# Head normalised tile by tile, query weights loaded in two parts, output matmuls started on their first inputs, and more zero-weight matmuls in a two-layer attention and gMLP kernel

## The chip, the cores and the metric

The kernel runs on one core of a Trainium2 chip. The metric is the device time of one launch in microseconds (us). I quote medians of several launches. One profiled launch per kernel gives the trace; its span is about 1.8 us shorter than the time of the same launch. TensorE runs the matmuls, whose results land in a memory called PSUM; ScalarE computes exponentials and other table functions, VectorE and GpSimd do elementwise work, and DMA queues move data. Copying a result out of PSUM is called eviction.

## The reference, cut to what matters

```python
# S = 2048 tokens, D = 512, H = 32 heads of Dh = 16, one shared K and one shared V head
def attention(x):                       # layernorm(x) comes in
    q, k, v = x @ wq, x @ wk, x @ wv
    p = softmax(q_h @ k.T * Dh**-0.5)   # 32 heads, 2048 x 2048 each
    return concat_heads(p @ v) @ wo
def mixer(x):                           # F = 1792, Fh = 896
    z = gelu(x @ w_in)
    z1, z2 = z[:, :Fh], layernorm(z[:, Fh:])
    g = w_sp @ z2 + b_sp[:, None]       # spatial 2048 x 2048 matmul ("gating")
    return (z1 * g) @ w_out
for _ in range(2):                      # two layers
    x = x + attention(layernorm(x))
    x = x + mixer(layernorm(x))
```

The work is dominated by 2 x 32 x 2048 x 2048 exponentials.

## The kernel before

The kernel builds a fixed instruction order for each engine, with its own list scheduler, before anything runs. The scheduler works with modelled durations and with the priorities in the code (a lower `prio` goes first); on the chip each engine runs its list in order and waits on semaphores. So a small edit of a priority or a dependency can move instructions far away from the place of the edit.

Most exponentials are computed on ScalarE, about 500 blocks of them on VectorE by a polynomial. After each chunk of queries ScalarE switches its function table to gelu and back; I call this a gelu stall. TensorE has a clock that drops after idle time (a stretch table below shows it fall to 0.50), and the kernel fills its idle time with matmuls whose weights are zero. I call the three places where the exponentials do not run back to back the seams: the head, the end of layer 0 and the end of layer 1.

The loading of the weights, with the clears of padded buffers on GpSimd (`pm` is a GpSimd memset):

```python
lq = self.dma(lambda e: e.dma_start(wq_nat, A_wq.rearrange(...)), (), "ldq", 524288, 1.2, "act")
for p in range(8):
    ld_x(p)                                   # 8 pairs of 128-row tiles of x, on the other queue
# ... cut ...
m = pm(self.wk_rep[:], 0.0, 512, 0.4)         # then a ScalarE copy of wk into it
m = pm(self.wv_rep[:], 0.0, 512, 0.5)         # then a ScalarE copy of wv into it
m = pm(self.wq_pad[:], 0.0, 4096, 0.6)
self.c_wq = sc.op("act", ... ACTF.Copy of all 2048 elements of wq ..., [m, lq], 1.2)
m = pm(self.V[:], 0.0, 2048, 0.7)
```

The keys: tiles are normalised two at a time, and all K and V matmuls of a pair are one job (`ln` also computes the reciprocal roots, on GpSimd):

```python
ts = (2 * p, 2 * p + 1)
ev = self.ln(ts, ...)
# ... cut ...
_, (k, v) = sc.job([(pe, 4 * d_mm(256) + 8 * d_mm(128))], [...], [ev, self.c_wk, self.c_wv], 1.0)
```

The end of a layer: for each of eight output blocks of 256 rows, gating matmuls for seven feature tiles in four groups, then eviction, addition and multiplication, then output matmuls that wait for all of them:

```python
for tc in range(8):
    hs = []
    for f0 in range(0, NF, 2):
        # ... gating matmuls (cut) ...
        pl, (ev,) = sc.job(pieces, [dict(... tensor_copy ..., prio=1.1, ...)], ...)
        ad = sc.op("dve", ... ALU.add ..., [ev] + ..., 0.9)
        ev = sc.op("dve", ... ALU.mult ..., [ad, zld], 0.9)
        hs.append(ev)
    for tt in range(2):
        ks = [(0, 1), (2, 3), (4, 5, 6)]
        pl, (xo,) = sc.job([... output matmuls, one piece for each of ks ...],
                           [... residual addition ...], hs + [self.l_wout], pr - 0.3)
```

The zero-weight matmuls: `peek` offers one only when the next unit of attention is neither at the end nor exactly at the half (the seam between the layers), and not before `wo` has been loaded:

```python
def peek(self, f):
    if u >= len(k.units) or u == len(k.units) // 2 or k.l_wo.start is None or k.c_zero.start is None:
        return None
    f = max(f, k.l_wo.vis, k.c_zero.vis)
```

The softmax here doesn't subtract the row's maximum and nothing guards it: scores larger than these inputs give would overflow.

## Time and profile before

The median of three launches was 1889.84 us (1886.19 to 1890.11).

| | of 1887.9 us |
|---|---|
| ScalarE busy | 93% |
| VectorE busy | 93% |
| TensorE busy | 85% |
| mean granted TensorE clock | 0.979 |
| first exponential | 18.3 us |
| last exponential of layer 0, first of layer 1 | 887.9, 932.7 us |
| last exponential of layer 1 | 1825.9 us |

These are whole lines of the page of the profile before: the busy times of the engines, the chain of work that ended last by engine, and two groups (ScalarE's exponentials and the zero-weight matmuls). In a group line the figures after the bar are busy us, mean ns of one, and the idle time before it with what ended it.

```profile
PE 1613.0 (85%) x12178; PEld 497.1 (26%) x12178; DVE 1750.5 (93%) x3129; ACT 1763.4 (93%) x1570; POOL 58.2 (3%) x101
...
ACT 35%; PE 26%; DVE 25%; issue 13%; POOL 1%; ACTq 0%; POOLq 0%
...
L1288 ACT ACTIVATE Pa<-ps_all 128x1536 bf16<-128x1536 f32 (+1 forms) x1440 | 1642.9, 1345 | 33.4 <-PE ps_all L1559 28.7
...
L1545 PE MATMUL ps_all<-wo_r,zero 128*128 128x512 bf16 x818 | 256.2, 391 | 0.6 <-DVE E L1464 0.2
```

Two engines are busy 93% of the time. Inside the attention the share is higher: from 100 to 200 us ScalarE is busy 100.0 us and VectorE 98.8. So the attention stretches are nearly full, but for the gelu stalls. What can be had without touching them is in the seams. The timeline of the head before (start us, length us, engine, line, operation, and in brackets the idle time before it with what ended it):

```profile
2.34 3.51 POOL L566 MEMSET wq_pad<- 128x4096 bf16 x1
...
5.79 1.80 POOL L566 MEMSET V<- 128x2048 bf16 x1
...
7.89 0.72 POOL L602 TENSOR_TENSOR rs<-ve,mhalf 128x2 f32<-128x2 f32 x1
...
10.08 1.91 ACT L582 ACTIVATE wq_pad<-z1s 128x2048 bf16<-128x2048 bf16 x1 [4.70 <-DMA z1s<-in_A_wq_dram]
...
14.63 3.28 PE L739 MATMUL ps_all<-xnTA,wq_pad 128*128 128x512 bf16 x8
...
18.29 2.36 ACT L1288 ACTIVATE Pa<-ps_all 128x1536 bf16<-128x1536 f32 x2 [1.11 <-PE ps_all L1559]
21.67 44.98 ACT L1288 ACTIVATE Pa<-ps_all 128x1536 bf16<-128x1536 f32 x39 [1.01 <-PE ps_all L1559]
```

GpSimd clears buffers until 7.6 us, and only then computes the first reciprocal root, on which the first normalised tile waits. The eight query matmuls take 3.28 us.

The chain of waits through the last seam before (start us, length us, engine, tile, line):

```profile
1837.06 3.18 PE ps_all L875 x8
...
1847.47 7.66 PE ps_all L1123 x28
...
1858.91 6.23 PE ps_all L1123 x28
1865.17 0.69 DVE X L1128
1865.86 0.60 DVE E L1102
1866.71 0.42 DVE E L1105
...
1868.59 0.30 DVE E L1108
1868.93 6.23 PE ps_all L1123 x28
```

L875 is a group of the last chunk's input matmuls, L1123 the output matmuls of two blocks. TensorE works 6.23 us, then waits 3.8 us through a chain of VectorE work, and the next two blocks begin 10.02 us after the last (1858.91 to 1868.93).

The stretch table around one gelu stall of layer 1 before. Of each line I use the stretch, its length, the first busy time (TensorE, with its count), the fourth (ScalarE) and the number before the last two, which is the granted clock:

```profile
1454.00:1462.00 8.00, 7.69 (x36) 3.25 (x34) 5.99 (x9) 7.99 (x4) 0.00 (x0) 1.00 0.01 2
1462.00:1465.00 3.00, 0.00 (x0) 0.00 (x0) 0.00 (x0) 3.00 (x1) 0.00 (x0) 0.95 0.00 0
1465.00:1470.00 5.00, 0.00 (x0) 0.00 (x0) 2.52 (x6) 4.97 (x3) 0.00 (x0) 0.50 0.33 107
```

The zero-weight matmuls of this stall run at its start, because nothing makes them wait. Then TensorE idles, from 1461.7 us on in the timeline, and some 3.0 us later its clock falls to half: the 0.95 is 2.7 us at full clock and 0.3 at half.

### The profile page before, as it was taken

The numbers are of one execution on the slowest core, as the hardware profiler recorded it, in microseconds if no ns is written. First come the engines' busy times: TensorE is split into PE (matmuls) and PEld (weight loads), VectorE is DVE, ScalarE is ACT, GpSimd is POOL, SyncE is SP. The second block draws the span as 40 slices with busy tenths as digits, with TensorE's granted clock in tenths as the row PEclk, the third lists the DMA queues.
The fourth block names the chain that finished last, engine by engine and source line by source line (L and its number), as shares of the span: only waits on it lengthen the run. The fifth ranks groups of instructions, "written<-read, shape, count | busy, mean of one in ns | idle before, by whom it ended". The sixth has DMA issues, their size and how long they took to land.

```text
span 1887.9 us, 30817 instructions
## 1 busy us (share of the span) xinstructions
PE 1613.0 (85%) x12178; PEld 497.1 (26%) x12178; DVE 1750.5 (93%) x3129; ACT 1763.4 (93%) x1570; POOL 58.2 (3%) x101
## 2 busy tenths in 40 slices
PE   7877888788889998989888778888888899999987
PEld 3222222122222232222432222222222223223233
DVE  7999999999889999997869999999999799989977
ACT  7999999999999999998579999999999999999973
POOL 3000000000000000000100000000000000000000
PEclk9999999999999999999999999999999799989999
DMA  9900000000010101011110000000000100011213
GB/s 254 232 1 1 1 1 1 1 1 1 5 36 23 46 1 43 24 55 45 54 33 1 1 1 1 1 1 1 1 1 1 40 23 23 1 43 35 66 45 109
DMA packets 85448, 59.17 MB, mean 31 GB/s; under 512 B 39476, under 2 KB 81720, under 8 KB 85304
## 3 DMA queue, kind: packets, MB, share of 16 engines
q1 hardware_dynamic: 83720, 56.64, 10.6%
q8 instruction: 97, 1.59, 0.4%
q10 hardware_dynamic: 1584, 0.56, 0.1%
q14 instruction: 47, 0.39, 0.1%
HBM read 30.97 MB, written 17.83 MB: 26 GB/s over the span
## 4 chain that ended last, share of the span: by engine, by line
ACT 35%; PE 26%; DVE 25%; issue 13%; POOL 1%; ACTq 0%; POOLq 0%
ACT Pa L1288 32%; PE ps_all L1036 7%; PE ps_all L1559 7%; PE ps_all L1363 4%; DVE E L1464 4%; DVE Pd L1502 3%; PE ps_all L1123 2%; DVE E L1500 2%; DVE E L1491 2%; DVE E L1497 2%; PE ps_all L1545 1%; DVE st L596 1%; ACT z2n L943 1%; DVE z2n L886 1%; DVE E L1494 1%
## 5 line engine op out<-in xcount | busy, mean ns | idle before, releaser
L1288 ACT ACTIVATE Pa<-ps_all 128x1536 bf16<-128x1536 f32 (+1 forms) x1440 | 1642.9, 1345 | 33.4 <-PE ps_all L1559 28.7
L1559 PE MATMUL ps_all<-qs,kT 32*128 32x512 bf16 x4096 | 567.9, 390 | 206.4 <-ACT Pa L1288 193.4
L1464 DVE TENSOR_SCALAR E<-ps_all 128x512 int32<-128x512 f32 x499 | 339.7, 684 | 24.0 <-PE ps_all L1559 22.5
L1559 PEld LDWEIGHTS ps_all<-qs,kT 32*128 32x128 bf16 x4096 | 139.4, 91 | 754.6 <-ACT Pa L1288 674.5
L1363 PE MATMUL ps_all<-Pa,V 128*32 128x512 bf16 x3597 | 324.3, 391 | 0.1
L1502 DVE SCALAR_TENSOR_TENSOR Pd<-E 128x1024 uint16<-128x1024 int32 x250 | 303.4, 1214 | 0.9
L1545 PE MATMUL ps_all<-wo_r,zero 128*128 128x512 bf16 x818 | 256.2, 391 | 0.6 <-DVE E L1464 0.2
L1036 PE MATMUL ps_all<-wsT,z2n 128*128 128x512 bf16 x714 | 198.9, 388 | 3.5 <-DVE gp L1048 2.4
L1363 PE MATMUL ps_all<-Pd,V 128*32 128x512 bf16 x499 | 176.6, 390 | 0.0
L1497 DVE TENSOR_TENSOR E<-E 128x1024 f16<-128x1024 f16 x250 | 170.9, 684 | 3.3
L1500 DVE TENSOR_TENSOR E<-E 128x1024 f16<-128x1024 f16 x250 | 170.4, 682 | 1.9
L1491 DVE TENSOR_SCALAR E<-E 128x1024 f16<-128x1024 uint16 x250 | 170.9, 684 | 1.3
L1493 DVE TENSOR_SCALAR E<-E 128x1024 f16<-128x1024 f16 x250 | 104.6, 418 | 2.2
L1494 DVE TENSOR_SCALAR E<-E 128x1024 f16<-128x1024 f16 x250 | 104.3, 417 | 2.1
L1545 PEld LDWEIGHTS ps_all<-wo_r,zero 128*128 128x128 bf16 x818 | 62.2, 97 | 132.1 <-issue 105.0
L1363 PEld LDWEIGHTS ps_all<-Pa,V 128*32 128x32 bf16 x3597 | 63.6, 94 | 121.5 <-issue 113.7
L1048 DVE TENSOR_TENSOR gp<-ps_all,gp 128x512 f16<-128x512 f32 x112 | 75.5, 685 | 20.3 <-PE ps_all L1036 20.0
L1036 PEld LDWEIGHTS ps_all<-wsT,z2n 128*128 128x128 bf16 x714 | 55.5, 98 | 100.3 <-issue 54.5
L739 PE MATMUL ps_all<-xnTA,wq_pad 128*128 128x512 bf16 (+2 forms) x384 | 71.0, 314 | 1.8 <-DVE E L1464 1.3
L875 PE MATMUL ps_all<-w_in_r,xnTB 128*128 128x448 bf16 x256 | 64.9, 365 | 4.6 <-DVE xnTB L628 1.7
L1123 PE MATMUL ps_all<-E 128*128 128x512 bf16 x224 | 55.2, 396 | 12.3 <-DVE E L1108 12.1
L911 PE MATMUL ps_all<-xnTB,w_in_r 128*128 128x512 bf16 (+2 forms) x336 | 61.8, 310 | 3.7 <-DVE z1s L922 1.9
(85 smaller groups left out, 1087.6 us busy)
## 6 DMA issues: line engine op xcount, KB each, us to landing
wsT_scratch<-gp SPq DMA_DIRECT2D x16, 512.0 KB, 4.0
wsT<-wsT_scratch SPq DMA_DIRECT2D x8, 1024.0 KB, 5.3
z1s<-z_scratch SPq DMA_DIRECT2D x16, 448.0 KB, 4.0
wsT<-wsT_scratch SPq DMA_DIRECT2D x8, 512.0 KB, 3.5
z_scratch<-z1s SPq DMA_DIRECT2D x4, 896.0 KB, 6.3
X<-in_A_x_dram SPq DMA_DIRECT2D x8, 256.0 KB, 7.5
out_dram<-X SPq DMA_DIRECT2D x16, 128.0 KB, 1.8
w_in_r<-in_B_w_in_dram SPq DMA_DIRECT2D x1, 1792.0 KB, 12.1
```

The source lines that it names most:

```text
L1036: ins = e.matmul(self.b32(b), self.z2n[:, s, f * 128:(f + 1) * 128], w_[:, s - s0, :], start=st, stop=sp)
L1288: return e.activation(k.Pa[:, base:base + n, :], k.b32(b0, n).rearrange("p (k q) -> p k q", k=n), ACTF.Exp, scale=SCALE)
L1363: ins = e.matmul(k.b32(k.pvb)[32 * j:32 * j + 32, :], k.V[:, u.kt, 32 * j:32 * j + 32], b.slot, tile_position=(0, 32 * j), start=u.first, ...
L1464: return k.sc.op("dve", lambda e: e.tensor_scalar(k.eI[:, s, 512 * i:512 * (i + 1)], k.b32(j.bank.idx)[:, 0:512], C_LOG2, C_BIAS, op0=ALU. ...
L1491: return lambda e: e.tensor_scalar(out, a, m, None, op0=ALU.mult)
L1493: return lambda e: e.tensor_scalar(out, a, b, None, op0=ALU.add)
L1494: return lambda e: e.tensor_scalar(out, a, m, b, op0=ALU.mult, op1=ALU.add)
L1497: o4 = sc.op("dve", lambda e: e.tensor_tensor(q, u, w, ALU.mult), d_sb(n, 0.521e-3), [o3], pr)
L1500: o6 = sc.op("dve", lambda e: e.tensor_tensor(q, q, u, ALU.mult), d_sb(n, 0.521e-3), [o5], pr)
L1502: o7 = sc.op("dve", lambda e: e.scalar_tensor_tensor(po.bitcast(U16), I, 2.0 ** -9, q, op0=ALU.mult, op1=ALU.add), d_sb(n, 1.042e-3), [o6] ...
L1545: return e.matmul(k.b32(k.pvb if b is None else b.idx), k.zero[:], k.wo_r[:, 0, :], start=b is not None, stop=b is not None)
L1559: return e.matmul(self.b32(bank), self.kT[32 * j:32 * j + 32, kt * 128:(kt + 1) * 128], self.qs[32 * j:32 * j + 32, g.q.slot, :], tile_pos ...
```

## The change

The intent is to shorten the three seams: start the exponentials sooner, keep TensorE's clock up where it had been left to fall, and let the output matmuls of a layer's end begin before all their inputs are there. The diff, cut to its core (cut are: lent PSUM banks at the start, the new helpers, the split of the K and V matmuls into two jobs for the first two pairs, query matmuls that wait for their own part of wq alone, and the addition of epsilon on VectorE instead of GpSimd in the normalisations at the ends of the layers):

```diff
 # load: wq in two parts, clears on VectorE (vm) instead of GpSimd (pm)
-lq = self.dma(... wq_nat ..., "ldq", 524288, 1.2, "act")
+lq = [ld_q(0, 128, "act")]
 for p in range(8):
     ld_x(p)
+    if p == 3:
+        lq.append(ld_q(128, 512, "sp"))
-m = pm(self.wq_pad[:], 0.0, 4096, 0.6)
-self.c_wq = sc.op("act", ... copy of 2048 elements ..., [m, lq], 1.2)
-m = pm(self.V[:], 0.0, 2048, 0.7)
+m = vm(self.wq_pad[:], 4096, 0.11)                       # wk_rep, wv_rep likewise
+c0 = rows(wqv[:, :, 0:8, :], wqn[:, :, 0:8, :], m, lq[0], 512, 1.2)               # ScalarE
+c1 = rows(wqv[:, :, 8:32, :], wqn[:, :, 8:32, :], m, lq[1], 1536, 3.0, "pool")    # GpSimd
+m = vm(self.V[:], 2048, 0.13)
 # layer_keys: the first four tiles one by one, first in priority
-ev = self.ln(ts, ..., 1.0)
+pr = 0.3 if p < 2 else 1.0
+for tt in ([ts[:1], ts[1:]] if p < 2 else [ts]):
+    evs.append(self.ln(tt, ..., dd, pr, p < 2))          # urgent: + eps on VectorE
 # closing: earlier block first, output matmuls start on the first feature tiles
-... prio=1.1 ... / 0.9 / 0.9
+... prio=1.1 + 0.01 * tc ... / 0.9 + 0.01 * tc / 0.89 + 0.01 * tc
-    dur=d_psum(512), prio=0.8, deps=[...])], hs + [self.l_wout], pr - 0.3)
+    dur=d_psum(512), prio=0.8, deps=[...])], [self.l_wout], pr - 0.3,
+    piece_deps=[hs[0:1], hs[1:2], hs[2:4]], soft=evs)
 # WarmStream.peek: also before the first scores and at the ends of the layers
-if u >= len(k.units) or u == len(k.units) // 2 or k.l_wo.start is None or k.c_zero.start is None:
+if sc.nleft == 0 or k.c_zero.start is None:
     return None
-f = max(f, k.l_wo.vis, k.c_zero.vis)
+f = max(f, k.c_zero.vis)
 # ... and the moving operand is zeros too, so wo need not have been loaded
-return e.matmul(..., k.zero[:], k.wo_r[:, 0, :], ...)
+return e.matmul(..., k.zero[:], k.zero[:, None, :].to_broadcast([P, 4, P]), ...)
```

## The prediction

> **What bounds the kernel now.** The page's busy table gives ScalarE 93% and VectorE 93% of 1887.9 us, TensorE 85%. The chain of waits gives ScalarE 35% (nearly all exponentials), TensorE 26%, VectorE 25%: two attention stretches in which exponentials run back to back (busy 99-100% in the stretch table), joined by three seams where they do not run: the head (0-22 us), the end of layer 0 (about 860-980) and the end of layer 1 (about 1825-1888). The change leaves the attention loop alone and works on the seams. By the instruction order VectorE's exponential blocks go from 499 to 497, zero-weight matmuls from 818 to 882.
>
> **Head.** In the timeline the first exponential starts at 18.3 us, with another ScalarE gap of 1.0 us ending at 21.7. The chain there is a 3.5 us clear of wq on GpSimd, a 1.8 us clear of V, which delays the first reciprocal root to 7.9 us, then pairwise normalisation, and a 1.9 us wq copy on ScalarE ending at 12.0, in front of the first key evictions. TensorE is cold: eight query matmuls take 3.28 us, 1.89 later. Now the clears move to VectorE before X lands (3.9 us), tiles go one at a time, only a quarter of wq is waited for, and fourteen zero-weight matmuls warm TensorE from about 1 us. My estimate from these durations: four tiles need some 1.3 us of VectorE each, so the last is ready near 10 us, then queries (1.8) and eviction (0.6): first exponential at 13-14 us. Gain about 5 us, and all later work shifts with it.
>
> **End of layer 1.** Each two output blocks take 10.02 us: output matmuls 6.23 busy, then 3.7 us of eviction, addition and multiplication during which TensorE waits. VectorE interleaves both blocks, so both become ready late. Now the earlier block has priority and output matmuls start on the first two feature tiles. VectorE work per two blocks, from issue spacing: 4.8 us of add and multiply, 2.4 of residual adds, 0.6 of eviction, 7.8 in all; TensorE needs about 7.6. I expect about 8.5 per two blocks, 5-6 us over four. The warm clock should bring the eight gating matmuls from 3.18 us (clock 0.67 there) to about 1.6, and the first output group from 7.66 to 6.2. Together about 8 us.
>
> **End of layer 0.** The same edits, but the gating matmuls are already warm (1.69) and VectorE is 97-100% busy during 915-925 with the next layer's statistics; the gain is the cold output group (7.90 us, clock 0.83) and earlier starts: about 3-4 us.
>
> **Not expected to change.** The gelu stalls: in 1450-1500 the clock is 0.80, because 34 zero-weight matmuls run at once and TensorE then idles 8.6 us. The change gives them no wait that would pace them. The Trainium skill ("TensorE: Matmul & The Clock Gate", section on what is happening) says about 3.4 us of idleness halves the clock; this trace agrees (0.50 from 1465).
>
> **Sum:** 5 + 8 + 3.5, about 16.5 us of 1890, less than 1%. I predict 1873 us, 80% range 1862 to 1883. Chances: faster by over 2% 0.03, within 2% 0.96, slower 0.01.
>
> **Shown right by:** first exponential at 13-14 us; matmuls before it at full clock; last output blocks every 8-9 us; gating matmuls of layer 1 near 1.6 us; unchanged clock dips at the gelu stalls; unchanged mean of exponentials.
>
> **Wrong if:** keys for later tiles arrive late and return the head's gain as ScalarE gaps before 40 us; the zero-weight matmuls delay real ones; GpSimd's long wq copy delays a reciprocal root or slows VectorE; or the reshuffled static order shifts the cold clock after gelu stalls by some us either way.

## The result, and the profile after

| | before | after |
|---|---|---|
| median, us | 1889.97 of 4 | 1877.49 of 4 |
| range, us | 1886.19 to 1890.75 | 1875.62 to 1878.77 |
| profiled launch: span, us | 1887.9 | 1873.8 |
| mean granted clock of it | 0.979 | 0.989 |

The ratio is 0.9937, with a 95% interval of 0.992 to 0.9954: within 2%, and faster by 12.5 us of the medians. A ratio here is the mean time of one kernel's runs over that of the other's of the same rounds, so it is not quite the ratio of the medians that I quote. The profiled launch of after was the fastest of its four, so the two spans differ by 14.1 us.

To see where the time came from, I cut both traces at ScalarE's exponentials: the start of the 41st (the start-up is over by then), the last of layer 0, the 41st of layer 1, the last of layer 1, and the end.

| stretch, us | before | after | difference, of unrounded times |
|---|---|---|---|
| head, to the 41st exponential | 64.9 | 60.9 | -4.0 |
| rest of layer 0's attention | 823.0 | 824.9 | +1.9 |
| seam between the layers, to the 41st exponential of layer 1 | 112.8 | 109.6 | -3.3 |
| rest of layer 1's attention | 825.2 | 823.7 | -1.5 |
| last seam | 62.0 | 54.8 | -7.2 |

The differences add up to -14.1. The three seams give 14.5 us, and the attention between them changes by +0.4 in sum. At the 41st exponential of the head both kernels have done the same work (100 blocks on ScalarE and 8 on VectorE), so the mark is fair. Head and last seam repeat within some tenths of a us between kernels that have the same order there; the attention stretches do not, and the seam between the layers moves by up to 4.0 us when only the head is edited (see the experiments).

The page of the profile after, the lines that answer to those of before:

```profile
PE 1609.1 (86%) x12242; PEld 498.9 (27%) x12242; DVE 1745.3 (93%) x3131; ACT 1764.5 (94%) x1580; POOL 53.4 (3%) x94
...
ACT 33%; DVE 28%; PE 25%; issue 13%; POOL 1%; ACTq 0%; POOLq 0%
...
L1319 ACT ACTIVATE Pa<-ps_all 128x1536 bf16<-128x1536 f32 (+1 forms) x1440 | 1643.1, 1355 | 29.4 <-PE ps_all L1591 21.7
...
L1577 PE MATMUL ps_all<-zero 128*128 128x512 bf16 x882 | 272.3, 391 | 4.8 <-DVE gp L1076 2.6
```

The exponentials' busy time is the same (1642.9 and 1643.1 us; the means of 1345 and 1355 ns count overlapping time twice). The time was not won in the main work. The timeline of the head after:

```profile
0.98 4.62 PE L1577 MATMUL ps_all<-zero 128*128 128x512 bf16 x14 [0.98 <-POOL zero L574]
...
1.49 1.76 DVE L582 MEMSET wq_pad<- 128x2048 uint32 x1 [0.37 <-issue]
...
6.10 1.08 POOL L617 TENSOR_TENSOR rs<-ve,mhalf 128x1 f32<-128x1 f32 x2 [1.05 <-DVE ve L615]
6.63 0.63 ACT L586 ACTIVATE wq_pad<-z1s 128x512 bf16<-128x512 bf16 x1 [0.84 <-DMA z1s<-in_A_wq_dram]
...
11.66 1.89 PE L766 MATMUL ps_all<-xnTA,wq_pad 128*128 128x512 bf16 x8
...
14.36 3.71 ACT L1319 ACTIVATE Pa<-ps_all 128x1536 bf16<-128x1536 f32 x3
```

The first reciprocal root starts at 6.10 instead of 7.89, the query matmuls at 11.66 instead of 14.63 and in 1.89 us instead of 3.28, the first exponential at 14.36 instead of 18.29. The clear of wq takes 1.76 us on VectorE, where it took 3.51 on GpSimd. It is not free: VectorE clears until 4.6 us, so the first tile's statistics start at 4.52 us, where before they started at 3.89.

The trace shows how TensorE's clock comes up in the head. The weight loads of the zero-weight matmuls start 0.43 us apart until 3.9 us; the next six fit into 1.18 us, so they are about 0.22 apart. The Trainium skill ("TensorE: Matmul & The Clock Gate", section "Wait — 56ns, not 53.3ns?") gives 426.7 ns cold and 215.7 ns warm from start to start for this shape, and this trace agrees. The clock column does not show it: it reads 1.00 from the first moment of both traces, so in the head one has to read the spacing. The moment is not fixed: with the clears on GpSimd (an experiment below) the zero-weight matmuls start at 0.98 us too, and the spacing falls only at 5.2 us.

The chain of waits through the last seam after. For the stretch in which the input matmuls (L902) run, 1829.99 to 1834.99 us, the chain names no releaser; in the timeline their eight take 1.68 us:

```profile
1831.60 1.68 PE L902 MATMUL ps_all<-w_in_r,xnTB 128*128 128x448 bf16 x8
```

The output blocks on the chain:

```profile
1847.55 1.87 PE ps_all L1153 x8
1849.46 3.20 PE ps_all L1153 x14
1852.65 0.44 PE ps_all L1120 x4
1853.09 1.29 PE ps_all L1153 x6
1854.39 0.23 PE ps_all L1120 x2
1854.67 0.69 DVE X L1158
1855.41 0.50 PE ps_all L1120 x3
1855.91 1.87 PE ps_all L1153 x8
```

Output matmuls (L1153, 28 for two blocks) now stand between gating matmuls (L1120). The long wait for VectorE is gone, and the period of two blocks is 8.36 us (1847.55 to 1855.91) instead of 10.02.

The stretch table of the same gelu stall after:

```profile
1453.00:1458.00 5.00, 2.21 (x11) 0.78 (x8) 0.22 (x1) 5.00 (x2) 0.00 (x0) 1.00 0.00 0
1458.00:1464.00 6.00, 0.65 (x7) 0.21 (x11) 3.43 (x9) 5.97 (x4) 0.00 (x0) 0.50 0.43 142
1464.00:1472.00 8.00, 7.96 (x44) 1.54 (x46) 5.59 (x14) 6.79 (x7) 0.00 (x0) 0.52 0.37 123
```

The stall is as cold as before. In sum over the trace the half-clock windows went from about 78 us to 41 us. Every one inside either trace is a multiple of 3.413 us long, within the rounding of the trace. The Trainium skill ("TensorE: Matmul & The Clock Gate", section "What's actually happening") gives 3413 ns for the window, calls it free-running and the clock binary. The trace agrees with the length and with the two values; stretches with 0.52 hold some of each. That the window runs free is not shown directly, but launches of one and the same kernel differ in their mean clock (0.975 to 0.985 for before), and the clock came up at 3.9 us in this head and at 5.2 in the other.

### The profile page after: what moved, and what is told of

Same layout as the page of the kernel before. It is cut to its first block, busy times and chain, and to the rows that moved or that the text cites. A ratio compares the mean times of both kernels' runs of the same rounds, so it can differ in the third digit from the quotient of the medians.

```text
span 1873.8 us, 30967 instructions
## 1 busy us (share of the span) xinstructions
PE 1609.1 (86%) x12242; PEld 498.9 (27%) x12242; DVE 1745.3 (93%) x3131; ACT 1764.5 (94%) x1580; POOL 53.4 (3%) x94
## 3 DMA queue, kind: packets, MB, share of 16 engines
q1 hardware_dynamic: 84248, 57.03, 10.6%
## 4 chain that ended last, share of the span: by engine, by line
ACT 33%; DVE 28%; PE 25%; issue 13%; POOL 1%; ACTq 0%; POOLq 0%
ACT Pa L1319 31%; PE ps_all L1064 7%; PE ps_all L1591 6%; DVE E L1496 5%; PE ps_all L1395 4%; DVE Pd L1534 3%; DVE E L1529 2%; DVE E L1532 2%; DVE E L1523 2%; PE ps_all L1153 2%; DVE st L611 2%; PE ps_all L938 1%; PE ps_all L902 1%; DVE E L1526 1%; DVE E L1525 1%
## 5 line engine op out<-in xcount | busy, mean ns | idle before, releaser
L1319 ACT ACTIVATE Pa<-ps_all 128x1536 bf16<-128x1536 f32 (+1 forms) x1440 | 1643.1, 1355 | 29.4 <-PE ps_all L1591 21.7
L1591 PE MATMUL ps_all<-qs,kT 32*128 32x512 bf16 x4096 | 564.0, 387 | 215.7 <-ACT Pa L1319 201.2
L1534 DVE SCALAR_TENSOR_TENSOR Pd<-E 128x1024 uint16<-128x1024 int32 (+1 forms) x249 | 301.9, 1212 | 0.5
L1577 PE MATMUL ps_all<-zero 128*128 128x512 bf16 x882 | 272.3, 391 | 4.8 <-DVE gp L1076 2.6
L1395 PE MATMUL ps_all<-Pd,V 128*32 128x512 bf16 x497 | 172.4, 387 | 0.0
L1529 DVE TENSOR_TENSOR E<-E 128x1024 f16<-128x1024 f16 (+1 forms) x249 | 169.7, 682 | 2.8
L1532 DVE TENSOR_TENSOR E<-E 128x1024 f16<-128x1024 f16 (+1 forms) x249 | 169.9, 682 | 2.1
L1523 DVE TENSOR_SCALAR E<-E 128x1024 f16<-128x1024 uint16 (+1 forms) x249 | 169.9, 682 | 1.3
L1526 DVE TENSOR_SCALAR E<-E 128x1024 f16<-128x1024 f16 (+1 forms) x249 | 104.1, 418 | 2.3
L1525 DVE TENSOR_SCALAR E<-E 128x1024 f16<-128x1024 f16 (+1 forms) x249 | 104.2, 419 | 2.0
L1577 PEld LDWEIGHTS ps_all<-zero 128*128 128x128 bf16 x882 | 67.3, 98 | 144.6 <-issue 109.1
L902 PE MATMUL ps_all<-w_in_r,xnTB 128*128 128x448 bf16 x256 | 62.9, 355 | 3.6 <-DVE xnTB L643 1.7
L989 DVE BATCH_NORM_STATS2 st<-z2n 128x6 f32<-128x448 bf16 x64 | 36.3, 600 | 22.4 <-ACT z2n L970 16.7
```

Of the source, the lines that this page charges most:

```text
L1319: return e.activation(k.Pa[:, base:base + n, :], k.b32(b0, n).rearrange("p (k q) -> p k q", k=n), ACTF.Exp, scale=SCALE)
L1395: ins = e.matmul(k.b32(k.pvb)[32 * j:32 * j + 32, :], k.V[:, u.kt, 32 * j:32 * j + 32], b.slot, tile_position=(0, 32 * j), start=u.first, ...
L1523: return lambda e: e.tensor_scalar(out, a, m, None, op0=ALU.mult)
L1525: return lambda e: e.tensor_scalar(out, a, b, None, op0=ALU.add)
L1526: return lambda e: e.tensor_scalar(out, a, m, b, op0=ALU.mult, op1=ALU.add)
L1529: o4 = sc.op("dve", lambda e: e.tensor_tensor(q, u, w, ALU.mult), d_sb(n, 0.521e-3), [o3], pr)
```

## The experiments

My theory was that each seam's gain comes from the part of the change that touches it, and that the parts of one seam are links of a chain. The rivals: that the whole gain is a side effect of a warmer clock, or of a luckier static order in the attention. Each kernel below is the changed kernel with one part undone, unless told otherwise. All gave correct outputs. "41st" is the start of the 41st exponential of the head.

### Head: one part undone at a time

The four kernels of this group ran on one chip beside three launches of the kernel before (median 1889.20).

**Pairs again.** The first four tiles are normalised two at a time, as before:

```diff
-for tt in ([ts[:1], ts[1:]] if p < 2 else [ts]):
+for tt in [ts]:
```

> The changed kernel with one thing undone: the first four tiles are normalised in pairs again, not one by one. Theory (the head is one chain of VectorE statistics, root, normalisation, transposes, and single tiles shorten it): a pair waits for one more tile of statistics (about 1.05 us), so the first exponential starts 0.7 to 1.5 us later than the 14.4 us of the changed kernel. Rival (wq or the clock sets the head, not the grouping of tiles): first exponential within 0.3 us of 14.4.

Measured: 1880.66 us (two launches), ratio to before 0.9959 (0.993 to 0.9988). First exponential 16.4 us (+2.0 against after), 41st 64.4 (+3.5). From its timeline:

```profile
13.91 1.67 PE L766 MATMUL ps_all<-xnTA,wq_pad 128*128 128x512 bf16 x7
...
16.40 3.71 ACT L1319 ACTIVATE Pa<-ps_all 128x1536 bf16<-128x1536 f32 x3
```

The matmuls are warm, but they start later: the first weight load of the eight is at 13.59 us, where after has 11.55, so 2.0 us later. (The trace holds seven of the eight matmuls; the missing record is the first, so 13.91 is the second's start.) Normalising by tile is worth more than I had expected.

**wq in one piece.** The whole of wq is loaded on the first queue and copied by ScalarE:

```diff
-lq = [ld_q(0, 128, "act")]
+lq = [ld_q(0, 512, "act")]
-        lq.append(ld_q(128, 512, "sp"))
-c0 = rows(wqv[:, :, 0:8, :], wqn[:, :, 0:8, :], m, lq[0], 512, 1.2)
-c1 = rows(wqv[:, :, 8:32, :], wqn[:, :, 8:32, :], m, lq[1], 1536, 3.0, "pool")
+c0 = rows(wqv, wqn, m, lq[0], 2048, 1.2)
```

> The changed kernel with wq loaded whole and copied whole by ScalarE again. Theory (the copy of all of wq, 1.9 us on ScalarE ending at 12.0 before, stood in front of the evictions): first exponential 1.5 to 3 us later than 14.4. Rival (the normalisation chain alone sets the start, and wq was ready in time either way): within 0.3 us of 14.4.

Measured: first exponential 15.2 us (+0.8), 41st 61.1 (+0.2). My expectation fell: once the other parts are there, loading wq in two parts is worth almost nothing. The two launches took 1881.99 us (clock 0.985) and 1895.73 (0.977), with one and the same instruction order. So the total of this kernel (ratio 1.0002, 0.9914 to 1.009) says nothing about the head. The profile fell on the slower launch, where layer 1's attention took 838.4 us (after 823.7).

**No zero-weight matmuls before the first scores.** They wait for `wo` again:

```diff
-if sc.nleft == 0 or k.c_zero.start is None:
+if sc.nleft == 0 or k.c_zero.start is None or k.l_wo.start is None:
-f = max(f, k.c_zero.vis)
+f = max(f, k.c_zero.vis, k.l_wo.vis)
```

> The changed kernel without zero-weight matmuls before the first scores (they wait for wo to be loaded, as before). Theory (a cold clock costs the key and query matmuls about twice their time: 3.28 against 1.89 us for the queries, 0.4 us for each group of four 128-column ones): first exponential 1.5 to 3 us later than 14.4. Rival (the real matmuls warm the clock in time, or TensorE is not on the chain): within 0.5 us.

Measured: 1879.12 us (two launches), ratio 0.9951 (0.9922 to 0.998). First exponential 15.0 us (+0.6), but 41st 63.6 (+2.7). From its timeline:

```profile
20.18 1.02 ACT L1319 ACTIVATE Pa<-ps_all 128x1024 bf16<-128x1024 f32 x1 [1.49 <-PE ps_all L1591]
```

Three exponentials run, then ScalarE waits 1.49 us for scores. A head must not be judged by its first exponential alone.

**Clears on GpSimd again.**

```diff
-m = vm(self.wk_rep[:], 512, 0.1)        # vm: VectorE; wv_rep, wq_pad and V likewise
+m = vp(self.wk_rep[:], 512, 0.4)        # vp: GpSimd
```

> The changed kernel with the clears of the four padded tiles on GpSimd again. Theory (clears of 3.5 and 1.8 us on GpSimd delay the first root, from about 6.1 to about 8 us): first exponential 1.5 to 2.5 us later than 14.4. Rival (on VectorE the clears delay the first statistics as much, 4.5 us where the data would allow 3.9, so nothing is gained by the move): within 0.5 us of 14.4.

Measured: 1890.58 us (two launches), ratio 1.0012 (0.9982 to 1.0041). First exponential 16.5 us (+2.1), 41st 65.1 (+4.2). GpSimd's clears end at 7.56 us and the reciprocal roots start at 7.53 instead of 6.10. The total is 13 us above after, of which the head explains 4.2: the attention took 830.7 us in layer 0 and 827.3 in layer 1, where after has 824.9 and 823.7. The edit touches only the head, so the rest of the difference is not its own effect: the order of what comes behind it changed.

The four losses at the 41st exponential (3.5, 0.2, 2.7 and 4.2 us) sum to 10.6, but the whole change gains 4.0 there. The parts are links of one chain: with any of three of them missing, most of the gain is missing.

These four kernels keep the change at the ends of the layers, and so serve as a check on the other marks. Their last seams are 53.6 to 54.8 us (after 54.8). But their seams between the layers are 113.6, 110.6, 109.3 and 111.0 us (after 109.6, before 112.8). The first of them, pairs again, is as slow there as before, with no half-clock window in that seam and no edit there. So a difference of 3 to 4 us in the seam between the layers can come from a reshuffled order alone.

### The ends of the layers

The kernels of this part, all but the second, ran on one chip beside seven launches of before (median 1888.50).

**The layer's end as before** (priorities and dependencies of the output matmuls reverted):

```diff
-... prio=1.1 + 0.01 * tc ... / 0.9 + 0.01 * tc / 0.89 + 0.01 * tc
+... prio=1.1 ... / 0.9 / 0.9
-    ... [self.l_wout], pr - 0.3, piece_deps=[hs[0:1], hs[1:2], hs[2:4]], soft=evs)
+    ... hs + [self.l_wout], pr - 0.3)
```

> The changed kernel with the output blocks at layer ends as before: no priority for the earlier block, output matmuls wait for all features. Measured by the seam from the last exponential to the end (62.0 us before, 54.8 changed) and by the period of two output blocks (10.02 before, 8.36 changed). Theory (the pipelining of addition, multiplication and output matmuls is most of the end's gain): period back to about 10.0, seam 59 to 61 us, time 4 to 6 us longer than the changed kernel's. Rival (the warm clock is most of it): seam below 56.5.

Measured: 1886.29 us (four launches), ratio 0.999 (0.996 to 1.002). Last seam 61.8 us (after 54.8), seam between the layers 113.1 (after 109.6). From its timeline:

```profile
1845.22 5.78 PE L1153 MATMUL ps_all<-E 128*128 128x512 bf16 x26
1850.84 2.04 PE L1120 MATMUL ps_all<-z2n 128*128 128x256 bf16 x14
...
1855.23 0.38 PE L1576 MATMUL ps_all<-zero 128*128 128x512 bf16 x1
1855.45 5.78 PE L1153 MATMUL ps_all<-E 128*128 128x512 bf16 x25
```

Again the output matmuls run in one block, then wait, and the period is 10.2 us. In the seam between the layers the first exponential of layer 1 even came earlier than in after (37.3 us after the last of layer 0, instead of 39.6), and the 41st came 3.5 us later. That is the same lesson as in the head.

**Only the dependencies reverted, priorities kept.** It ran beside seven other launches of before (median 1888.79):

```diff
-    ... [self.l_wout], pr - 0.3, piece_deps=[hs[0:1], hs[1:2], hs[2:4]], soft=evs)
+    ... hs + [self.l_wout], pr - 0.3)
```

> The changed kernel with one half of the end's pipelining undone: the earlier block keeps its priority, but output matmuls wait for all seven features again. Theory (VectorE's interleaving of two blocks was the fault, so the priority does most of it): period of two output blocks 8.4 to 9.0 us (8.36 changed, 10.02 before), last seam 55 to 57 us. Rival (starting on the first two features is what fills TensorE's wait): period 9.3 to 10.0, seam 58 to 61.

Measured: 1885.95 us (four launches), ratio 0.999 (0.9968 to 1.0013), last seam 61.8, seam between the layers 113.0: the same as with both reverted. The priorities alone are worth nothing. The gain in the last seam needs the earlier start of the output matmuls; the earlier start without the priorities was not run. I had named both in the prediction, and given the priorities a part. In the seam between the layers the loss of 3.5 us is no larger than what an edit of the head alone did there, so nothing is shown for it. The run also speaks against the rival of the warmer clock: its profiled launch has the same mean clock as after's, 0.989, and lacks the gain of 8.5 us (by medians).

**No zero-weight matmuls at the ends of the layers.**

```diff
-if sc.nleft == 0 or k.c_zero.start is None:
+if sc.nleft == 0 or k.c_zero.start is None or u >= len(k.units) or (u == len(k.units) // 2):
```

> The changed kernel without zero-weight matmuls at the two layer ends (those before the first scores stay). Theory (they keep the clock at full through the gating matmuls and the first output group, worth 2 to 3.5 us in the last seam): seam from the last exponential to the end 57 to 58.5 us against 54.8, gating matmuls near 3.2 us again, cold windows after the last exponential. Rival (the denser output blocks keep TensorE warm by themselves): seam 54.5 to 55.5.

Measured: 1882.64 us (four launches), ratio 0.9974 (0.9944 to 1.0004). Last seam 56.1 us (+1.3, less than expected), seam between the layers 111.8 (+2.2). The input matmuls in its timeline, and then its stretch table there:

```profile
1836.66 3.17 PE L902 MATMUL ps_all<-w_in_r,xnTB 128*128 128x448 bf16 x8 [0.69 <-ACT xnTB L644]
```

```profile
1836.00:1840.00 4.00, 3.34 (x14) 1.56 (x15) 0.63 (x1) 1.27 (x3) 0.00 (x0) 0.57 0.00 0
```

The matmuls take 3.17 us instead of 1.68, which is 1.5 us, and the seam loses 1.3. So in this seam the zero-weight matmuls are worth some 1.3 us and the dependencies 7.0, each measured with the other in place. (The 2.2 in the seam between the layers is again within what a reshuffle does.)

**Both undone.**

> Both undone together: output blocks as before and no zero-weight matmuls at layer ends. Theory (the two parts add up, and only the epsilon additions on VectorE stay of the change to the ends): last seam 61 to 62 us, as before the change (62.0), seam between the layers 43.5 to 45 (44.8 before). If the parts don't add up, the seam lies well below the sum of the two single reversals.

Measured: 1897.29 us (1895.43 to 1904.62, four launches), ratio 1.0055 (1.002 to 1.0091), so slower than before. The last seam was 60.2 us, not the 63.1 that the two losses would add up to, and no half-clock window fell into it. The seam between the layers was 121.2 us, with a window of 10.2 us from 993 us on. The losses do not add. The output matmuls in its timeline:

```profile
1867.99 6.22 PE L1153 MATMUL ps_all<-E 128*128 128x512 bf16 x27 [1.91 <-DVE E L1138]
...
1878.00 6.22 PE L1153 MATMUL ps_all<-E 128*128 128x512 bf16 x27 [1.91 <-DVE E L1138]
```

By chance this run settles how the last seam's gain divides. It has the layer's end as before at full clock and without zero-weight matmuls. Against before (62.0, with two half-clock windows of 3.4 us there) it is 1.9 us shorter: that is mainly the cold clock of before, with the epsilon additions and small differences of order in it. Against after (54.8) it is 5.4 longer: that is the later start of the output matmuls. The 7.0 above is larger because the run with the layer's end as before keeps its zero-weight matmuls. It too is at full clock, yet 1.6 us longer than this one; 0.9 of that lies in the four output groups, where a zero-weight matmul stands among the output matmuls (1855.23 above) and the period is 10.2 us instead of 10.0. So zero-weight matmuls can delay real ones. The other 0.7 lies before the output blocks and is not explained.

**No early load of the exponential table in the last layer.** This is an addition to the changed kernel. In the last layer no exponential follows:

```diff
-pre = sc.op("act", lambda e: e.activation(self.tiny[:], self.mhalf[:], ACTF.Exp), ..., table="exp")
+if g.layer == 0:
+    sc.op("act", ... the same ...)
```

> The changed kernel without the table load for exponentials in the last layer's end, where no exponential follows (1.28 us on ScalarE between the first eviction of gated features and the next ones). Theory (it stands on the chain: the first output matmuls waited for ScalarE's evictions): last seam 53.0 to 53.8 us against 54.8, all before it unchanged. Rival (VectorE is the limit there and ScalarE has slack): 54.5 to 55.

Measured: last seam 54.0 us (-0.8, less than expected), 1877.10 us (four launches), ratio 0.9938 (0.9903 to 0.9974). The total can't be told from after's. The trace has the table load at 1.28 us. The Trainium skill ("ScalarE: Activation LUTs", section "What ACT_TABLE_LOAD costs") gives about 1283 ns, which agrees, and some 1380 ns of drain on top, which this trace does not show: in the kernel before, the exponentials end at 854.79 us, the load starts at 854.80 and the gelu at 856.10, so the switch took 1.31 us.

### The cold clock after gelu stalls

The change left these alone, and about 41 us at half clock remained. Over the 27 launches of before that ran beside the experiments, time and mean granted clock have a correlation of -0.95, and the fitted slope is 1.25 us for each 0.001 of clock. If that held across kernels, filling the windows would be worth several us more.

**Pacing, first try.** A tiny gelu starts a chain of GpSimd operations, and the zero-weight matmuls wait for the latest one of the chain:

```diff
+anc = sc.op("act", ... a tiny Gelu ..., -1.0, table="gelu")
+for _ in range(int((gdur + 1.3) / 1.2)):
+    pv = sc.op("pool", ... power of 128 x 4 numbers ..., 1.2, [pv, ...], -1.0)
+    self.pace.append(pv)
-o = k.sc.op("pe", fn, 512 / 2400.0, [k.c_zero] + ..., 9.0, sem="warm")
+o = k.sc.op("pe", fn, 512 / 2400.0, [k.c_zero] + pd + ..., 9.0, sem="warm")    # pd: latest pace
```

> The changed kernel plus a pacer: during each gelu stall GpSimd runs a chain of small power operations that starts with the stall, and each group of zero-weight matmuls waits for one of them, so that they are spread over the stall and don't run at once. Theory (half-clock windows after gelu stalls, 41 us of them in the changed kernel's trace, and some 1.2 us of time per 0.001 of mean clock between runs of the kernel before, cost the attention stretches time): the windows at 506, 854 and 1458 us vanish or shrink to one of 3.4 each, mean granted clock 0.993 or more, time 4 to 10 us below the changed kernel's 1877.5. Rival (the stretches are bound by ScalarE and VectorE, and the clock only goes along with other disturbance): clock up, time within 2 us of 1877.5.

Measured: 1914.86 us (four launches), ratio 1.0133 (1.011 to 1.0157). The kernel was flawed: the scheduler put exponentials between the tiny gelu and the real one, with two extra table loads at a stall. The run says nothing of the pacing.

**Pacing, mended.** The tiny gelu gets a higher priority than the real one, so that nothing comes between, the real one waits for its own inputs again (cut here), and the chain fits the measured durations:

```diff
-anc = sc.op("act", ..., -1.0, table="gelu")
+anc = sc.op("act", ..., -1.1, table="gelu")
-for _ in range(int((gdur + 1.3) / 1.2)):
+for _ in range(int((gdur + 2.6) / 1.12)):
```

> The pacer again, mended: in the first attempt the small activation that marks the start of a gelu stall was separated from the gelu by exponentials, which added two table loads to each stall (some 20 us over the kernel) and started the pacer too early, so it decided nothing. Now it stands directly in front of the gelu, and the chain of power operations (about 1.1 us each in that trace) lasts through the whole stall. No table load is added. Theory (half-clock windows after gelu stalls cost the attention stretches time): the windows of 10.2, 10.2 and 13.7 us after the stalls shrink to 3.4 or less, mean granted clock 0.993 or more, time 4 to 10 us below the changed kernel's 1877.5. Rival (ScalarE and VectorE bound the stretches whatever the clock): clock up, time within 2 us of 1877.5.

Measured: 1872.05, 1877.61, 1877.60 and 1877.58 us, ratio 0.9944 (0.991 to 0.9978; worked back from the mean of the four, it rests on one launch of before, of 1886.77). The stretch table of one gelu stall of layer 1, and the group of the chain:

```profile
1432.00:1438.00 6.00, 3.64 (x21) 0.86 (x21) 2.88 (x5) 5.99 (x4) 4.26 (x4) 1.00 0.00 0
1438.00:1442.00 4.00, 2.85 (x10) 0.65 (x10) 0.00 (x0) 4.00 (x2) 3.74 (x4) 1.00 0.00 0
1442.00:1448.00 6.00, 3.89 (x14) 0.96 (x14) 2.36 (x6) 5.97 (x3) 5.34 (x6) 1.00 0.25 79
```

```profile
L984 POOL TENSOR_TENSOR pc<-pc,mhalf 128x4 f32<-128x4 f32 x56 | 61.5, 1099 | 230.3 <-ACT tiny L979 226.5
```

The pacing works: the stall is at full clock, half-clock windows fall from 41 to 17 us, the mean clock is 0.995 in the profiled launch. Layer 0's attention gains 7.3 us (817.6 for 824.9). But 2.8 us come back in the seam between the layers (112.4 for 109.6), 0.6 in the last seam, layer 1's attention gains nothing (824.0), and the median is that of after. These stretches are of the fastest launch, the profiled one; the other three were 5.5 us slower, and they have no trace. So the slope found within one instruction order does not carry over to another. Why layer 1 gains nothing with a full clock is not settled; the order changed too.

**The mended pacing and no early table load together**, five rounds:

> The two additions that each did no harm, together: the changed kernel with the mended pacer and without the last layer's table load. Up to the last seam its instruction order is that of the paced kernel. Theory (the last seam is one chain, so 0.8 us less there shows in the total): last seam 54.3 to 54.8 us against 55.4 in the paced kernel, median 1875.5 to 1877.0, mean 1 to 2 us below the changed kernel's 1877.3, half-clock windows 30 us or less in all. Rival (the spread from run to run, 1872 to 1878 with one and the same order, is larger than both and hides them): median 1877 to 1878.

Measured: 1874.34 us (1871.52 to 1878.19), ratio 0.993 (0.9917 to 0.9944); last seam 54.5 us, layer 0's attention 818.1. It has the lowest median of all, 3.2 us below after's, but the two ranges overlap. It was run at another time. I do not call it faster than after.

## Why the prediction was right, point by point

The prediction was right: 1873 us with a range of 1862 to 1883, "within 2%" at 0.96, against 1877.49 us and "within 2%". The gain was 12.5 us by medians and 14.1 between the two profiles, where the sum had 16.5. The mechanism held for the head and the last seam; for the seam between the layers it is not shown, and the gelu stalls did not stay as predicted.

- *What bounds the kernel.* The prediction said that the attention stretches are full and that the gain lies in the seams. The traces show 14.5 us from the seams, and +0.4 net from the rest.
- *Head, predicted about 5 us, first exponential at 13 to 14.* Measured 4.0 us and 14.36. The term was over-sized by 1. I had the fourth tile ready near 10 us and then the queries. The tile was normalised at 10.17, about as predicted, but I had left out its transposes and their copy, which end at 11.15; the queries start at 11.66. The undone parts show that tiles one by one, clears on VectorE and the early warm clock are all needed. The part for loading wq in two was wrong: 0.2 us.
- *End of layer 1, predicted about 8 us.* Measured 7.2. The period is 8.36 us where I had 8.5, the input matmuls (which the prediction calls gating matmuls) take 1.68 us where I had 1.6. At one and the same full clock the earlier start gave 5.4 us, where I had 5 to 6, and the cold clock of before cost 1.9, where I had about 3 (1.6 in the input matmuls and 1.5 in the first output group). The mechanism was half wrong in its naming: it needs the start on the first feature tiles, and the priority of the earlier block alone gives nothing.
- *End of layer 0, predicted 3 to 4 us.* Measured 3.3 at the 41st exponential. At the first exponential the seam is 5.3 us shorter, and 2 us of it are given back within the next 40. That the edits there are the cause is not shown: a kernel with all of them, and pairs again in the head, has 113.6 us here (before 112.8). The number may be luck.
- *Gelu stalls unchanged.* This failed in part. The half clock after the stalls at 504 and 1454 us of before stayed at 10.2 and 13.7 us, but after the one at 855 it grew from 6.8 to 10.2, and after the one at 1660 its 10.2 us are gone. The sum of all windows was halved, which I had not predicted and for which no run shows the cause, and the attention stretches did not become shorter for it.
- *What could go wrong.* The reshuffled order moved the attention by +1.9 and -1.5 us. It could have been much more: over the experiments, leaving the flawed pacing aside, layer 0's attention took between 817.6 and 830.7 us, and edits of the head alone moved it between 823.1 and 830.7. The prediction's range was wide enough for that, and its hit owes something to it. How much of after's own total is a lucky order can't be told from these runs.

The terms sum to 16.5 us and measured 14.5 in the seams. The difference is the head (1.0), the end of layer 1 (0.8) and the end of layer 0 (0.2). The last 1.6 us between the profile's gain and the medians' are spread from launch to launch: the profile of after was its fastest launch.

## What to carry to other kernels

When the main loops are full, cost a change by the seams: take the durations there, and judge a seam by a later mark (here the 41st exponential) rather than by the first instruction, since an early start is often given back. Starting a long consumer on the first pieces of its input gained most (5.4 us in one seam, at full clock in both kernels), while priorities alone did nothing. In a kernel with one static order, an edit's total holds its own effect plus a reshuffle of several us, so read an effect from its own stretch of the trace and not from the total, and check with edits made elsewhere that the stretch holds still without it: the last seam did within 1.2 us, the seam between the layers moved by 4.0.

## What the Trainium skill lacked or had wrong

- "TensorE: Matmul & The Clock Gate" does not say whether matmuls of zeros on zeros count as activity for the clock gate. They do: 14 of them from 0.98 us on bring the spacing from 0.43 to 0.22 us by about 3.9 us (in another run by about 5.2).
- The same page advises (section "Why this matters for your kernels") no idle gaps over about 3 us, and does not say how dense the filling must be. With paced zero-weight matmuls TensorE was busy 61% of a 6-us stretch (3.64 of 6.00, with ends of matmuls that the profile models) and kept clock 1.00. Filling matmuls without a wait all ran early and left 8.6 us idle and the clock at 0.50.
- No page says what a cold window costs in a kernel that TensorE does not bound. Within one order 27 launches give 1.25 us for each 0.001 of mean clock; across orders it did not hold (half-clock windows from 41 to 17 us left the median at 1877.6).
- "ScalarE: Activation LUTs", section "What ACT_TABLE_LOAD costs", has about 2.66 us for a switch of tables with its drain. In this trace a switch took 1.31 us from the end of one activation to the start of the next, and leaving one out gained 0.8 us.
- "VectorE: DVE Perf Modes", section "Zero memsets can be issued as uint32 (trn2)", agrees as to the form: the 128x4096 bf16 clear appears as 2048 uint32 elements. The clear takes 1.76 us on VectorE. The page does not set this beside GpSimd's clear of the same buffer, 3.51 us here.
- No page has the duration of a small power on GpSimd, on which the reciprocal roots of a normalisation wait: 128x4 took 1.10 us, and the 128x2 in this kernel's head 0.72, as far as the profile's rough spans on GpSimd tell.
